# Banded attention and gated MLP on one core: convolution sums moved into PSUM, one schedule for the whole run, first probabilities turned by TensorE

## The chip, the cores and the metric

The kernel runs on one core of one Trainium2 chip. The metric is the device time of one execution in microseconds (us), lower is better. Three runs of the kernel before took 585.83, 588.0 and 584.61 us, median 585.83. Engines are called as the profile calls them: PE (TensorE; PEld its weight loads), DVE (VectorE), ACT (ScalarE), POOL (GpSimd), SP (the queue that issues all DMAs here).

## What is computed

Attention with 8 batches, 8 heads, 576 tokens and head size 64. Half of the heads see the last 32 positions, the other half the positions of equal remainder modulo 32. Its output goes through a gated MLP: 512 to 1024 features, a convolution of three taps along the tokens whose sigmoid gates the hidden value, and back to 512.

```python
scores = scale * np.matmul(q, k.transpose(0, 1, 3, 2))
scores = np.where(masks[None, :, :, :], scores, -1000000000.0)
attn = np.exp(scores - max); attn = attn / (sum + 1e-09)
x = np.matmul(attn, v)                        # heads side by side: (8, 576, 512)
h = np.maximum(x @ w_in, 0.0)                 # (8, 576, 1024)
conv_out += conv_w[k][None, None, :] * hp[:, k:k + S, :]   # k = 0, 1, 2; hp is h with a zero row at both ends
gate = 1.0 / (1.0 + np.exp(-conv_out))
return (h * gate @ w_out).astype(np.float32)
```

## The kernel before

**Attention.** Heads are worked in pairs, four pairs a batch; "head" below means such a pair. One head is: `scores` (L307, 36 small products into a PSUM tile of 128 x 576), row maximum and subtraction on DVE (L319, L320), exponential on ACT (L322), sum and reciprocal on DVE (L323, L325), scaling on POOL (L326, `pn`), a transposition of 32 x 32 blocks into `pt` (one DVE instruction for all blocks, L329, whose pieces ACT then copies to their places, L341; or DVE block by block, L344), `values` (L350, 18 products into the same PSUM tile), and a split of the result into a high part `xh` (ACT, L364) and a remainder `xl` (DVE, L365).

**MLP.** Products are made three times (high x high, high x low, low x high). `mm1` (L387) makes for each of 8 feature blocks f two halves of 288 tokens, 12 matmuls each, so 24 matmuls a block and 192 a batch. ACT clips them into `h` (L393). The convolution of a block is ACT's scaling (L398, `c`), two DVE multiply-adds (L404), ACT's sigmoid (L407), and the product with `h` (L409, DVE or in the first batch mostly POOL). The result is split into `gh` (ACT, L277) and `gl` (POOL or DVE by the string `SPLIT_G`, L280). `mm2` (L426) makes 4 x 2 output tiles out of all 8 blocks, 24 matmuls each, 192 a batch; ACT copies them out (L432) and SP stores them. So no output tile can end before the last block's `gl`.

**Weights.** The weights arrive as 64-bit words, in 16 chunks of 512 KB. Each chunk is turned into f32 by one ACT instruction (L245), five DVE instructions (L246 to L254) and one of POOL (L256), and then split into high and low (L277, L280; engine by `SPLIT_W`). `w_in` is done in the first stage and beside it, `w_out` behind it.

**Buffers.** Convolution sums `c` are three SBUF tiles. In a first stage four heads of batch 0 have four sets of attention buffers and four PSUM tiles `sF` of their own. Then that stage's pools are given back, and the second stage has two sets, two PSUM tiles `s` for attention and four `m` for matmuls. Each is a tile of its own.

**Order.** A class `Plan` records every operation with its engine, a duration, a due time and the keys that it reads and writes. `order` picks, engine by engine, the ready operation with the smallest due time, and the instructions are issued in that order, each engine in its own. The layer below (Tile) then sets the semaphore waits between engines from what each instruction reads and writes in the tiles; an engine that waits holds all that is queued behind.

Of the kernel before, what the change touches and what calls it, by code (L numbers as in the profile page):

```python
# [19 lines left out]
P = 128  # L20
# [4 lines left out]
WAIT = 0.1  # L25
ACT_PENALTY = 0
PE_PENALTY = 1

FIRST = "q0 q1 w0 q3 v1 w1 w2 q2 w3 v2 v3 c0 v0"
SETUP = ['vav', 'v', 'ava', 'v']  # L30
WARM = 4
WARM_SCORES = [2, 4, 2, 4]
WARM_VALUES = [0, 5, 0, 9]
FIRST_AT = [19.3, 22.4, 23.0, 26.9]
SECOND_AT = [11.6, 24.2, 37.3, 76.0]
LATER_AT = [31.8, 33.4, 39.2, 37.7]
START = 28.0
PERIOD = 70.0
MM1_STEP = 3.5
MM2_AT = 39.3  # L40
MM2_STEP = 22.4
LOAD_Q = 82.1
LOAD_V = 20.4
W_IN_AT = [-37.0, 3.8, 71.4, 61.1, 22.5, 42.2, 40.1, 48.5]
W_OUT_AT = [1.2, -51.9, 2.7, -37.4, 27.2, 25.2, 41.3, 30.0]
SPLIT_W = "pppppppvppvppvpv"
SPLIT_G = "vppvpppp"
FIRST_SCALE = "aavaaaav"
FIRST_GATE = "vppppvpp"


class Plan:
# [6 lines left out]
    def op(self, engine, dur, at, fn, reads=(), writes=(), chain=(), table=None):  # L59
        i = len(self.ops)  # L60
        deps = set(chain)
        for key in reads:
            if key in self.last_write:
                deps.add(self.last_write[key])
        for key in writes:
            deps.update(self.readers.get(key, ()))
            if key in self.last_write:
                deps.add(self.last_write[key])
        for key in reads:
            self.readers.setdefault(key, set()).add(i)  # L70
        for key in writes:
            self.last_write[key] = i
            self.readers[key] = set()
        deps.discard(i)
        self.ops.append((engine, dur, at, fn, deps, table))
        return i

    def order(self, free, done):
        ops = self.ops
        n = len(ops)  # L80
        left = [0] * n
        users = [[] for _ in range(n)]
        ready = [0.0] * n
        end = {}
        lo = len(done)
        for i in range(lo, n):
            for d in ops[i][4]:
                if d < lo:
                    ready[i] = max(ready[i], self.after(done[d], d, i))
                else:  # L90
                    left[i] += 1
                    users[d].append(i)
        pool = {}
        for i in range(lo, n):
            if not left[i]:
                pool.setdefault(ops[i][0], []).append(i)
        out = []
        while True:
            best = None
            for e, c in pool.items():  # L100
                if not c:
                    continue
                t = max(free.get(e, 0.0), min(ready[i] for i in c))
                def key(i):
                    sw = e == "act" and ops[i][5] not in (None, self.table) or e == "pe" and ops[i][5] != self.kind
                    return (ops[i][2] + (ACT_PENALTY if e == "act" else PE_PENALTY) * sw, i)
                cand = min((i for i in c if ready[i] <= t), key=key)
                for i in c:
                    if ready[i] > t and key(i) < key(cand) and ready[i] < t + min(WAIT, 0.9 * ops[cand][1]):
                        cand = i  # L110
                        t = ready[i]
                        break
                if best is None or t < best[0]:
                    best = (t, e, cand)
# [4 lines left out]
            if e == "act" and ops[i][5] not in (None, self.table):  # L119
                self.table = ops[i][5]  # L120
                t += 1.29
            if e == "pe" and ops[i][5] != self.kind:
                self.kind = ops[i][5]
                t += 0.087
            end[i] = t + ops[i][1]
            free[e] = end[i]
            out.append((t, i))
            for u in users[i]:
                ready[u] = max(ready[u], self.after(end[i], i, u))
                left[u] -= 1  # L130
                if not left[u]:
                    pool.setdefault(ops[u][0], []).append(u)
        out.sort()
        return [i for _, i in out], end

    def after(self, t, d, i):
        a, b = self.ops[d][0], self.ops[i][0]
        if a == "dma":
            return t + 0.92
        if b == "dma":  # L140
            return t + 1.25
        if a == b:
            return t if a == "pe" else t + 0.13
        if b == "pe":
            return t + 0.15
        return t + (0.2 if a == "pe" else 0.15 if a == "act" else 0.08 if a == "pool" else 0.2 if b == "pool" else 0.13)

    def emit(self, free, done):
        order, end = self.order(free, done)
        for i in order:  # L150
            self.ops[i][3]()
        done.extend(end[i] for i in range(len(done), len(self.ops)))
# [3 lines left out]
def tile_banded_attention_gated_mlp(ctx, tc, qT, kT, vw, w_in, conv, w_out, mask, ident, out):  # L156
# [24 lines left out]
    tt = const.tile([P, NU, 64], F32, name="tt")  # L181
# [6 lines left out]
    NW = 2  # L188
    words = [const.tile([P, 4, P, 2], I32, name=f"ws{i}") for i in range(NW)]
    wa = [const.tile([P, 4 * P], I32, name=f"wa{i}") for i in range(NW)]  # L190
    wt = [const.tile([P, 4 * P], I32, name=f"wt{i}") for i in range(NW)]
# [4 lines left out]
    def slot(n):  # L196
        return n if n < NHP else n % NB

    def load_q(n, at):
        i, b, hp = slot(n), n // NHP, HPS[n % NHP]  # L200
        q, k = buffers[i][:2]
# [357 lines left out]
```

## Time and profile before

| what | value |
|---|---|
| median of 3 runs | 585.83 us |
| the profiled execution | 583.28 us, of which 581.5 us are its span |
| DVE busy | 416.1 us (72%) |
| ACT busy | 348.6 us (60%) |
| POOL busy | 169.2 us (29%) |
| mean granted TensorE clock | 0.944 |
| HBM read, written | 41.79 MB, 9.44 MB |

The page gives busy time by engine, the span in 40 slices, the DMA queues, the chain of work that ended last, and groups of instructions by line. A group's row holds its busy time, the mean of one instruction, and the idle time of the engine just before, with what ended it. A row of the stretches ("windows") holds start and end, length, then busy time and number of instructions by engine, the granted clock, and the share and rate of DMA.

### The profile page before, as it was taken

The page shows a single profiled execution, that of the slowest core. Times are in us where ns is not written, and L with a number is a line of the kernel's source. Part 1 is how long each engine was busy: PE and PEld are TensorE (multiplying, and loading weights), DVE is VectorE, ACT ScalarE, POOL GpSimd, SP SyncE. Part 2 cuts the span into 40 slices and gives each one's busy share as a digit, 9 for nine tenths or more (in the row PEclk, how much of TensorE's full clock was granted, in tenths as well). Part 3 has the DMA queues.
Part 4 walks back from the last instruction along what each step waited for, and adds up shares of the span by engine and source line. Part 5 has one row for each costly group of instructions (what it writes and reads, how often), then busy time and mean ns, then how long its engine had stood idle before and what let it go on. Part 6 is the DMA issues. An engine that isn't in the chain of part 4 may idle for free.

```text
span 581.5 us, 15083 instructions
## 1 busy us (share of the span) xinstructions
PE 523.2 (90%) x6558; PEld 498.2 (86%) x6558; DVE 416.1 (72%) x587; ACT 348.6 (60%) x661; POOL 169.2 (29%) x148
## 2 busy tenths in 40 slices
PE   5468855798998999999999999999999999899997
PEld 2348854697997999999998999899999999799997
DVE  5596999998697666875787678767777668733830
ACT  4395685566676448663874477545765386535731
POOL 5434676674023111321033012311232103300220
PEclk9566967889999999999999999999999999999999
DMA  8994213445202460066006530355015600210001
GB/s 194 228 214 108 66 56 110 141 145 163 68 1 81 130 160 1 4 182 163 24 1 143 151 77 2 85 152 134 1 32 155 165 22 1 83 42 22 1 35 47
DMA packets 24178, 52.19 MB, mean 90 GB/s; under 512 B 2480, under 2 KB 10736, under 8 KB 24112
## 3 DMA queue, kind: packets, MB, share of 16 engines
q1 hardware_dynamic: 24112, 51.23, 33.0%
q8 instruction: 51, 0.84, 0.6%
q14 instruction: 15, 0.12, 0.1%
HBM read 41.79 MB, written 9.44 MB: 88 GB/s over the span
## 4 chain that ended last, share of the span: by engine, by line
PE 44%; DVE 22%; ACT 11%; issue 4%; POOL 0%; POOLq 0%; DVEq 0%; ACTq 0%
PE m L426 24%; PE m L387 13%; DVE c L404 8%; DVE c L409 6%; PE s L307 4%; ACT c L398 4%; ACT gh L277 2%; PE s L350 2%; ACT c L407 2%; DVE gl L280 1%; DVE wt L250 1%; DVE xl L365 1%; ACT pt L341 1%; ACT h L393 1%; ACT xh L364 1%
## 5 line engine op out<-in xcount | busy, mean ns | idle before, releaser
L387 PE MATMUL m<-xh,wil 128*128 128x288 f32 x512 | 153.1, 299 | 5.7 <-DVE wil L280 3.8
L426 PE MATMUL m<-gl,woh 128*128 128x288 f32 x512 | 153.7, 300 | 3.7 <-POOL gl L280 3.3
L426 PE MATMUL m<-gh,wol 128*128 128x288 f32 x512 | 152.6, 298 | 4.9 <-DVE wol L280 2.9
L426 PE MATMUL m<-gh,woh 128*128 128x288 f32 x512 | 155.5, 304 | 1.3 <-issue 1.3
L387 PE MATMUL m<-xh,wih 128*128 128x288 f32 x512 | 153.4, 300 | 2.0 <-DVE xl L365 1.5
L404 DVE SCALAR_TENSOR_TENSOR c<-h,cw,c 128x576 f32<-128x576 f32 x128 | 121.1, 952 | 44.7 <-ACT c L398 44.4
L387 PE MATMUL m<-xl,wih 128*128 128x288 f32 x512 | 153.1, 299 | 0.0
L280 POOL TENSOR_TENSOR gl<-c,gh 128x576 fp32r<-128x576 f32 x48 | 71.5, 1490 | 202.0 <-ACT gh L277 192.1
L426 PEld LDWEIGHTS m<-gl,woh 128*128 128x128 f32 x512 | 97.4, 190 | 9.1 <-POOL gl L280 7.5
L387 PEld LDWEIGHTS m<-xh,wil 128*128 128x128 f32 x512 | 98.2, 192 | 6.1 <-DVE wil L280 4.0
L426 PEld LDWEIGHTS m<-gh,wol 128*128 128x128 f32 x512 | 97.5, 190 | 4.0 <-DVE wol L280 3.4
L426 PEld LDWEIGHTS m<-gh,woh 128*128 128x128 f32 x512 | 97.3, 190 | 4.2 <-issue 1.5
L387 PEld LDWEIGHTS m<-xh,wih 128*128 128x128 f32 x512 | 98.2, 192 | 2.8 <-DVE xl L365 1.7
L387 PEld LDWEIGHTS m<-xl,wih 128*128 128x128 f32 x512 | 98.1, 192 | 0.0
L341 ACT COPY pt<-tt 32x288 f32<-32x288 f32 x160 | 68.8, 430 | 24.8 <-DVE tt L329 16.1
L326 POOL TENSOR_TENSOR pn<-t,sm 128x576 f32<-128x576 f32 x32 | 38.2, 1203 | 145.7 <-DVE sm L325 141.6
L277 ACT CAST gh<-c 128x576 fp32r<-128x576 f32 x64 | 43.0, 671 | 41.0 <-DVE c L409 39.3
L409 DVE TENSOR_TENSOR c<-h,c 128x576 f32<-128x576 f32 x58 | 54.7, 944 | 15.0 <-ACT c L407 14.1
L393 ACT ACTIVATE h<-m 128x288 f32<-128x288 f32 x128 | 50.5, 405 | 22.6 <-PE m L387 21.3
L432 ACT COPY o<-m 128x288 f32<-128x288 f32 x64 | 24.8, 398 | 58.5 <-PE m L426 54.2
L407 ACT ACTIVATE c<-c 128x576 f32<-128x576 f32 x64 | 43.4, 678 | 11.7 <-DVE c L404 11.0
L398 ACT ACTIVATE c<-h,cw 128x576 f32<-128x576 f32 x62 | 48.1, 775 | 1.5
(71 smaller groups left out, 590.2 us busy)
## 6 DMA issues: line engine op xcount, KB each, us to landing
v<-in_dram SPq DMA_DIRECT2D x32, 432.0 KB, 4.0
q<-in_dram SPq DMA_DIRECT2D x32, 288.0 KB, 5.0
k<-in_dram SPq DMA_DIRECT2D x32, 288.0 KB, 5.7
out_dram<-o SPq DMA_DIRECT2D x32, 288.0 KB, 2.2
ws<-in_dram SPq DMA_DIRECT2D x16, 512.0 KB, 3.7
k<-in_dram SPq DMA_DIRECT2D x1, 304.0 KB, 6.7
small<-in_dram SPq DMA_DIRECT2D x1, 32.0 KB, 2.1
cwords<-in_dram SPq DMA_DIRECT2D x1, 24.0 KB, 10.6
```

Of the source, the lines that this page charges most:

```text
L277: op(A, ta, at, lambda: nc.scalar.copy(hi(), src), [skey], [(key, "h")])
L280: lambda: eng.tensor_tensor(out=lo(), in0=src, in1=hi().bitcast(F32), op=ALU.subtract),
L326: op(G, 1.11, at + 5.5, lambda: nc.gpsimd.tensor_tensor(out=pn, in0=t, in1=sm.unsqueeze(2).to_broadcast([P, NU, 64]), op=ALU.mult), [("t", ...
L341: op(A, 0.333, at + 7.5, lambda dst=dst, j=j, p=p: nc.scalar.copy(dst, tt[j:j + 32, :, 32 * p:32 * p + 32]), ["tt"], [key])
L387: nc.tensor.matmul(ps, a[:, c, fs], x[:, c, tok], start=(n == 0 and m == 0), stop=(n == NC - 1 and m == 2))
L393: op(A, 0.291, at + 1.5 * t + 1.7, lambda ps=ps, t=t: nc.scalar.activation(out=h[:, 1 + t * H2:1 + t * H2 + H2], in_=ps, func=AF.Relu), [( ...
L398: op(A, 0.67, at + 3.6, lambda: nc.scalar.activation(out=c_, in_=h[:, 0:S], func=AF.Copy, scale=cw[:, f:f + 1]), kh + ["cw"], [kc])
L404: op(V, 0.73, at + 3.6 + 0.8 * kk, lambda kk=kk: nc.vector.scalar_tensor_tensor(out=c_, in0=h[:, kk:kk + S], scalar=cw[:, kk * NF + f:kk * ...
L407: op(A, 0.57, at + 6, lambda: nc.scalar.activation(out=c_, in_=c_, func=AF.Sigmoid), [kc], [kc], table=1)
L409: op(ge, 0.67 if ge == V else 1.36, at + 6.7, lambda: (nc.vector if ge == V else nc.gpsimd).tensor_tensor(out=c_, in0=h[:, 1:S + 1], in1=c ...
L426: nc.tensor.matmul(ps, a[:, f, ms], g[:, f, tok], start=(f == 0 and n == 0), stop=(f == NF - 1 and n == 2))
L432: op(A, 0.291, at + 3 * t + 3, lambda ps=ps, tok=tok: nc.scalar.copy(o[:, tok], ps), [("M", mi)], [("o", oi, t)])
```

## The change

1. **One PSUM tile `four`** of five banks (128 x 2560 f32) replaces the PSUM tiles of attention and the SBUF tiles `c`. It is cut into four regions of 576 columns and a spare of 256. A region is longer than a bank of 512 columns, so that neighbours share a bank. Regions 0 and 1 hold the scores and values of the heads (0 to 3 for the first batch), regions 2 and 3 by turns the convolution sums. Matmul tiles `m` fall from four to three.
2. **One schedule.** There is no first stage any more: all pools are opened at the start, attention has two sets of buffers from the first head on, and one plan covers the run. `h`, the gate's results `gt` and the output tiles lie in one SBUF tile `misc`, whose space the first three weight chunks use before.
3. **Turning by TensorE.** For the four heads of batch 0 and the first two of batch 1, POOL writes the probabilities between zero columns (`pad`), 18 matmuls with a shifted unit matrix put them transposed into PSUM, in three groups (eight into the head's region, four into the spare, six into the region again), and ACT copies each group to `pt`. L329 and eight L341 copies a head go, and the eight clearings of `pt` on POOL.
4. **The gate.** Where POOL makes the remainder, DVE writes the gate's result to SBUF (`gt`); elsewhere it stays in PSUM and DVE makes the remainder. POOL makes no gate any more.
5. **The plan** has new durations, models a port that DVE and POOL hold in turn (`lock`), the clock of TensorE and the rate of DMA, and has new due times and new strings for who splits what. It has no rule for two operations in different regions of `four`.

```diff
-FIRST = "q0 q1 w0 q3 v1 w1 w2 q2 w3 v2 v3 c0 v0"
+FIRST = "w1 w2 k0 w0 q0 q3 k1 q1 k2 v1 q2 w3 w4 c0 k3 v0 v2 v3"
...
-SPLIT_W = "pppppppvppvppvpv"
-SPLIT_G = "vppvpppp"
...
-FIRST_GATE = "vppppvpp"
+SPLIT_W = "vvpvvpvvpppvpvvv"
+SPLIT_G = "ppvvpppv"
+FIRST_SPLIT_G = "vpvppppv"
+TURNED = 2
...
+                if ops[i][6]:
+                    lock["dve"] = end[i] + 0.03
+                    lock["pool"] = end[i]
...
+    NHB, NGT, NPM = 3, 2, 3
+    misc = mlp.tile([P, NHB * (S + 2) + (NGT + 2) * S], F32, name="misc")
...
+    four = psum.tile([P, 5 * 512], F32, name="four")
+    spare = four[:, 4 * S:5 * 512]
+    psR = [four[:, S * i:S * i + S] for i in range(4)]
+    psM = [psum.tile([P, 512], F32, name=f"m{i}") for i in range(NPM)]
...
+    def region(n):
+        return n if n < NHP else n % 2
...
+    def turn(n, ps, ks, u0, n_u, key, at):
+        i = slot(n)
+        pt = buffers[i][3]
+
+        def turns():
+            for u in range(n_u):
+                for e in range(2):
+                    o = ps[0:96, 128 * u:128 * u + 128].rearrange("p (h x) -> p h x", h=2)[:, :, 32 * e:32 * e + 32]
+                    nc.tensor.matmul(o, pad[:, u0 + u, 32 - 32 * e:128 - 32 * e], unit[:, e, :], start=True, stop=True)
+        op(T, 0.112 * 2 * n_u, at, turns, ["tt", "unit"], [ks], table=3)
+        op(A, 0.25 + 0.105 * n_u, at + 0.5, lambda: nc.scalar.copy(
+            pt[:, :, u0:u0 + n_u, :].rearrange("p h u c -> p u h c"),
+            ps[0:96, 0:128 * n_u].rearrange("p (u h c) -> p u h c", h=2, c=64)), [ks], [key])
...
-        si = n if n < NHP else n % len(psum)
-        ps = psum[si][:, :S]
-        ks = ("S", si, n < NHP)
+        ps = psR[region(n)]
+        ks = ("R", region(n))
...
-        h, c_ = hs[hi], cs[hi]
+        h, gt, c_ = hs[hi], gts[gi], psR[ci]
+        sg = FIRST_SPLIT_G[f] if early else SPLIT_G[f]
...
-        kc = ("c", hi)
+        kc = ("R", ci)
...
+        if sg == "p":
+            op(V, 0.752, at + 6.7, lambda: nc.vector.tensor_tensor(out=gt, in0=h[:, 1:S + 1], in1=c_, op=ALU.mult), kh + [kc], [("gt", gi)] + old(gt0 + S * gi, S))
+            split(lambda: gh[:, f, :], lambda: gl[:, f, :], gt, at + 7.5, ("gt", gi), ("g", f), "p", 0.67, 0.752, 1.4, True)
+        else:
+            op(V, 0.752, at + 6.7, lambda: nc.vector.tensor_tensor(out=c_, in0=h[:, 1:S + 1], in1=c_, op=ALU.mult), kh + [kc], [kc])
+            split(lambda: gh[:, f, :], lambda: gl[:, f, :], c_, at + 7.5, kc, ("g", f), "v", 0.64, 0.752, 1.4, False)
```

What the built programs say of two places follows; the brackets name the semaphores for which an instruction waits, by the engine (or DMA queue) that raises them.

The first place is ACT in the convolution of a later batch. Before, the scaling of a block's neighbour (`c_541`, `c_542`) waits for ACT's own `h` and for POOL, which read that tile a batch ago:

```order
L398 ACTIVATE c_540<-h_537,cw 128x576 [waits Activation_49,Pool_49]
L393 ACTIVATE h_538<-m_552 128x288 [waits PE_49]
L407 ACT_TABLE_LOAD
L407 ACTIVATE c_540<-c_540 128x576 [waits DVE_49]
L393 ACTIVATE h_538<-m_553 128x288 [waits PE_49]
L393 ACTIVATE h_539<-m_550 128x288 [waits PE_49]
L398 ACTIVATE c_541<-h_538,cw 128x576 [waits Activation_49,Pool_49]
```

After the change the same engine stands so at that place (`misc` holds `h`, and `gt` where it is cast to `gh`):

```order
L542 ACTIVATE four<-four 128x576 [waits DVE_49]
L528 ACTIVATE misc<-m_95 128x288 [waits PE_49]
L533 ACTIVATE four<-misc,cw 128x576 [waits DVE_49]
L528 ACTIVATE misc<-m_96 128x288 [waits PE_49]
L387 CAST gh<-misc 128x576 [waits Pool_49]
L533 ACTIVATE four<-misc,cw 128x576 [waits DVE_49,Activation_49]
L528 ACTIVATE misc<-m_94 128x288 [waits PE_49]
L542 ACTIVATE four<-four 128x576 [waits DVE_49]
```

Each scaling L533 now waits for DVE: by the semaphore's value for DVE's last instruction on `four`, which worked on the other block's region. The same holds in the whole program. Taken in the order in which they are issued, the accesses to `four` change engine 399 times, and each time the later one waits, directly or through another wait, for the one ahead, whichever regions the two are in, and also where both only read.

The second place is PE in the first 30 us. Before, the scores of the four first heads stand next to each other, in tiles of their own:

```order
L307 MATMUL sF_114<-k_59,q_58 32x64 x36
L307 MATMUL sF_115<-k_67,q_66 32x64 x36
L307 MATMUL sF_117<-k_107,q_106 32x64 x36
L307 MATMUL sF_116<-k_99,q_98 32x64 x36
```

After, scores (L430) and turning matmuls (L412) alternate in `four`, and a first one of nearly each group waits for DVE or ACT:

```order
L430 MATMUL four_93<-k1_67,q1_66 32x64 [waits DMAHW1_49,DMAHW7_49,DMAHW0_49,DVE_49]
L430 MATMUL four_93<-k1_67,q1_66 32x64 x35
L412 MATMUL four_93<-unit_75,pad_74 96x2x32 [waits DMAHW2_49,Pool_49]
L412 MATMUL four_93<-unit_75,pad_74 96x2x32 x7
L430 MATMUL four_93<-k0_59,q0_58 32x64 [waits DMAHW5_49,DMAHW4_49]
L430 MATMUL four_93<-k0_59,q0_58 32x64 x35
L412 MATMUL four_93<-unit_75,pad_74 96x2x32 [waits Activation_49]
L412 MATMUL four_93<-unit_75,pad_74 96x2x32 x3
L412 MATMUL four_93<-unit_75,pad_74 96x2x32 [waits DVE_49]
```

The second head's scores wait for DVE's subtraction on the first head's region; the third and fourth groups of turning matmuls are held by ACT's copy and by DVE's maximum of other regions.

More of the change, by code (lines that the diff above doesn't have):

```diff
@@ L74, in op, with order @@
         deps.discard(i)
-        self.ops.append((engine, dur, at, fn, deps, table))
+        self.ops.append((engine, dur, at, fn, deps, table, lock))
         return i
-    def order(self, free, done):
+    def order(self, at):
         ops = self.ops
         n = len(ops)
-        left = [0] * n
-        users = [[] for _ in range(n)]
+        left = [len(o[4]) for o in ops]
+        users = self.users
         ready = [0.0] * n
[L84 to L94, printed above, removed]
-            if not left[i]:
-                pool.setdefault(ops[i][0], []).append(i)
+        pool = {e: [] for e in ("dma", "act", "dve", "pool", "pe")}
+        for i in range(n):
+            if not left[i]:
+                pool[ops[i][0]].append(i)
+        free = dict.fromkeys(pool, 0.0)
+        free["dma"] = 0.7
+        lock = {"dve": 0.0, "pool": 0.0}
+        moved = 0.0
+        idle, hot = 0.0, 0.0
+        table = kind = None
+        begin, end = [0.0] * n, [0.0] * n
@@ new lines, in best @@
+    def best(self):
+        n = len(self.ops)
+        self.users = [[] for _ in range(n)]
+        for i in range(n):
+            for d in self.ops[i][4]:
+                self.users[d].append(i)
+        rank = [o[2] for o in self.ops]
+        found = self.order(rank)
+        for _ in range(PASSES):
+            late = self.latest(rank)
+            order, begin, end = self.order(late)
+            if max(end) < max(found[2]):
+                found = order, begin, end
+            rank = end
+        return found
@@ L312, in warm_s @@
                 for _ in range(WARM_SCORES[n]):
[L313 to L316 removed]
+                    nc.tensor.matmul(psM[2][:, 288:], warm_[:, :P], warm_[:, :224], start=True, stop=True)
@@ L333, in attention @@
+        for h in range(0 if turned else 2):
             for e in range(2):
@@ new lines, in mm2, with warm_up @@
+        op(Q, 288, at + 6, lambda: nc.sync.dma_start(out=out[ms, b * S:(b + 1) * S], in_=o), [("o", oi, 0), ("o", oi, 1)], [])
+    warm_ = const.tile([P, 256], BF16, name="warm")
+    def warm_up():
+        nc.vector.memset(warm_, 0.0)
+        for _ in range(WARM):
+            nc.tensor.matmul(psM[2][:, 288:], warm_[:, :P], warm_[:, :224], start=True, stop=True)
+    with tc.manual_schedule():
+        op(T, 0.2 * WARM, -10, warm_up, (), [])
+        op(Q, 64, -19.9, lambda: nc.sync.dma_start(out=unit, in_=eye), (), ["unit"])
+        op(G, 0.4, -4.2, lambda: (nc.gpsimd.memset(pad[:, :, 0:32], 0.0), nc.gpsimd.memset(pad[:, :, 96:128], 0.0)), (), ["zero"])
+        op(Q, 32, -50, lambda: nc.sync.dma_start(out=small[D:], in_=ident), (), ["small"])
+        first = FIRST.split()
+        place = {tok: n - 20 for n, tok in enumerate(first)}
+        for j in range(NHP):
+            load_q(j, place["q%d" % j])
+            if j < NB:
+                set_up(j, place["k1"] - 0.5)
+            load_k(j, place["k%d" % j])
+            load_v(j, place["v%d" % j])
+            attention(j, FIRST_AT[j], None)
+        convert_conv(place["c0"])
+        for tok in first:
+            if tok[0] == "w":
+                convert_w_in(int(tok[1:]), W_IN_AT[int(tok[1:])], place[tok])
```

427 lines of the change are left out of this document (235 added, 192 removed).

## The prediction

> **What bounds the kernel now.** I read the share of each engine first, then the slices, then the chain that ended last.
>
> ```profile
> PE 523.2 (90%) x6558; PEld 498.2 (86%) x6558; DVE 416.1 (72%) x587; ACT 348.6 (60%) x661; POOL 169.2 (29%) x148
> PE   5468855798998999999999999999999999899997
> PEclk9566967889999999999999999999999999999999
> ```
>
> From the thirteenth slice (about 175 us) PE is full at full clock; before, it has gaps and a lowered clock. So there are two stages. The stretches give the first one's engines, and mm1's own stretches its start in batches 0 and 1.
>
> ```profile
> 30.00:40.00 10.00, 8.31 (x91) 5.80 (x93) 9.24 (x18) 9.34 (x21) 5.01 (x6) 0.53 1.00 216
> 90.00:100.00 10.00, 5.19 (x23) 4.96 (x23) 10.00 (x14) 7.14 (x13) 7.14 (x4) 0.66 0.30 84
> 230.00:300.00 70.00, 68.84 (x875) 67.11 (x874) 52.10 (x75) 44.63 (x86) 15.04 (x12) 1.00 0.29 78
> ...
> 40.00:50.00 10.00, 1.96 (x8) 1.96 (x9) 0.64 0.44 122
> 90.00:100.00 10.00, 5.19 (x23) 4.96 (x23) 0.66 0.30 84
> 140.00:150.00 10.00, 0.89 (x7) 1.01 (x8) 1.00 0.48 130
> ```
>
> At 90 us DVE is busy without a gap (weight chunks) and PE makes 23 matmuls in 5.19 us, 0.226 each, at clock 0.66. mm1 of batch 0 begins at 50 - 1.96 = 48.0, that of batch 1 at 150 - 0.89 = 149.1. From there the chain shows one period a batch:
>
> ```profile
> 214.24 12.73 PE m L387 x96
> ...
> 242.30 0.03 issue
> ...
> 244.41 0.74 DVE c L404
> 245.15 0.02 issue
> ...
> 249.32 1.58 PE s L307 x97
> ...
> 251.97 10.50 PE m L426 x78
> 262.47 2.25 PE s L350 x72
> 264.72 3.38 PE m L426 x24
> 268.11 2.15 PE s L307 x144
> 270.25 6.55 PE m L426 x48
> ...
> 525.59 12.74 PE m L387 x96
> ...
> 561.14 16.72 PE m L426 x124
> 577.86 0.02 issue
> ```
>
> mm1 starts at 214.24 and five batches later at 525.59: a period is 311.35 / 5 = 62.3 us. In it a matmul takes 12.73 / 96 = 0.1326 us, mm1 25.5. At 249.32, 35.1 us after mm1's start, the convolution of all blocks and the last `xl` are through and PE goes on; until then it has 25.5 us of mm1, 42 matmuls of mm2 (5.6) and two heads' values (2.25), so it idles some 1.8 us. Behind that point 27.5 us of PE work follow almost without a gap. **PE bounds the period; the convolution, alternating between ACT and DVE, ends just early enough.** That margin is what the change touches.
>
> The run before is thus 149.1 + (214.24 - 149.1) + 311.35 + (581.5 - 525.59) = 149.1 + 65.1 + 311.35 + 55.9 = 581.5 us, plus 1.8 outside the span.
>
> **The change, term one: a period.** After it every use of `four` by another engine waits for the use issued ahead. So a period's convolution is one chain through ACT and DVE, without the overlap of neighbouring blocks. Its pieces:
>
> ```profile
> L398 ACT ACTIVATE c<-h,cw 128x576 f32<-128x576 f32 x62 | 48.1, 775 | 1.5
> L404 DVE SCALAR_TENSOR_TENSOR c<-h,cw,c x128: 800/815/1856, 56.4 to 555.9; 128x576 f32<-128x576 f32 x128
> L407 ACT ACTIVATE c<-c x64: 667/680/691, 60.8 to 556.7; 128x576 f32<-128x576 f32 x64
> L409 DVE TENSOR_TENSOR c<-h,c x58: 742/756/1853, 62.6 to 557.4; 128x576 f32<-128x576 f32 x58
> L277 ACT CAST gh<-c x64: 657/674/679, 63.8 to 558.9; 128x576 fp32r<-128x576 f32 x64
> L280 DVE TENSOR_TENSOR gl<-c,gh x16: 746/758/1707, 66.6 to 546.6; 128x576 fp32r<-128x576 f32 x16
> L393 ACT ACTIVATE h<-m 128x288 f32<-128x288 f32 x128 | 50.5, 405 | 22.6 <-PE m L387 21.3
> ```
>
> A block whose remainder POOL makes: scaling 0.775, a multiply-add 0.815 and a second behind it 0.74 (chain), sigmoid 0.68, gate 0.756, and four hand-offs of 0.03 (the chain's "issue" rows): 3.89 us. Where DVE makes it, the cast 0.674 and the remainder 0.758 with two hand-offs join: 1.49 more. mm1 makes a block in 24 x 0.1326 = 3.18, so the chain, not mm1, sets the pace. By the new string these are blocks 2, 3 and 7. The chain begins when the first `h` is there, 3.18 + 0.405 + about 0.2 after mm1's start: 3.8. Eight blocks: 31.1; blocks 2 and 3: 3.0; gives 37.9. In block 7 a head's values or scores stand between the cast and the remainder in the issue order: 0.67 + 1.12 (2.25 / 2) + 0.76 + hand-offs with PE, say 0.3: 2.85. So the last `gl` lands **40.7 us** after mm1's start, against 35.1.
>
> What is queued behind: PE's mm2 needs block 5, 6 and 7 in turn, and PE does everything in order. The first 45 mm2 matmuls (6.0) and mm1 (25.5) fit before 40.7; PE idles there 8 us. Behind stand 147 matmuls at 10.50 / 78 = 0.1346, 19.8 us, four scores at 2.15 / 2 = 1.08 and three values at 1.12, 7.7 us, and I put 2 us for scores that wait, in `four`, for the other head's `xh` and `xl`. Sum: **70.2 us**, against 62.3 (bounds 66 and 74: the waits of the second half vanish and the values stand elsewhere, 3 to 4 less; or each of the seven costs 0.5 more). Batches 1 to 6: 6 x 70.2 = 421 against 65.1 + 311.35 = 376.5: **+45**. The last batch has no attention behind it: 3.8 + 31.1 + 3.0 + 1.5 = 39.4, then 138 matmuls (18.6) and the tail of 581.5 - 577.86 = 3.6: 61.6 against 55.9, **+6**.
>
> PSUM operands: the trace has no multiply-add on PSUM; subtracting and remaindering from PSUM take as long as from SBUF:
>
> ```profile
> L320 DVE TENSOR_TENSOR t<-s,mx 128x576 f32<-128x576 f32 x28 | 21.1, 755 | 0.7
> L365 DVE TENSOR_TENSOR xl<-s,xh 128x576 fp32r<-128x576 f32 x28 | 21.1, 754 | 25.5 <-ACT xh L364 24.8
> ```
>
> so I leave 0.815. An ACT or DVE that is 0.05 faster or slower per instruction moves the chain by 2 us, which the bounds hold.
>
> **Term two: the first stage.** Attention of batch 0 and of the first two heads of batch 1 lies in `four` too, in one chain.
>
> ```profile
> L307 PE MATMUL sF<-k,q x288: 216/254/317, 6.5 to 26.0; 128*32 128x64 f32 x144
> 50.00:60.00 10.00, 2.15 (x72) 1.91 (x72) 0.85 0.48 114
> 60.00:70.00 10.00, 1.21 (x72) 1.05 (x72) 1.00 0.16 54
> 30.00:40.00 10.00, 5.15 (x82) 4.62 (x84) 0.53 1.00 216
> ...
> L341 ACT COPY pt<-tt 32x288 f32<-32x288 f32 x160 | 68.8, 430 | 24.8 <-DVE tt L329 16.1
> ```
>
> Scores take 2.15 or 1.21 (second and third row, slow and full clock), values 5.15 x 36 / 82 = 2.26 or 1.12, maximum and subtraction 1.51, `xh` and `xl` 1.39. Turning is not in the trace: 18 matmuls, between the 18 of values (1.12) and twice 18 full-width ones at the slow clock, 36 x 0.226 = 8.1; I take 3.5 at the low clock and 2 at the full one, near the values. Its three copies lie between L341's 0.43 and `gh`'s 0.67 each; 1.5 together. Hand-offs of ten changes, many with PE, 1.2. A head: 13.5 at the low clock, 9.8 at the full. In this stage the clock was 0.50 to 0.66 before, and PE stays sparse, so I take 13.5. Four heads and two without `xh`, `xl` (12.1): 78 us. The first scores began at 6.5 us; now some 2.2 MB (three weight chunks among them) stand ahead of them in SP's queue, at 216 GB/s 10 us, so 13. mm1 of batch 0, but for single matmuls between, begins at **91** instead of 48. Then eight blocks with three DVE remainders (31.1 + 4.5), and among them two heads' `xh`, `xl`, scores (5.5) and those DVE weight instructions that stand in the chain (about 8): 49. Then the rest of mm2 and of two heads, on PE 141 x 0.1346 + 4.5 = 23.5, on DVE about 30 with five weight chunks: 28. mm1 of batch 1 begins at 91 + 49 + 28 = **168** against 149.1: +19. Bounds: all at the full clock, 13 + 56 + 43 + 24 = 136; slow turning and DVE held by POOL, 190.
>
> **What costs nothing or is hidden.** POOL loses six gates, six weight remainders and eight clearings; it is idle most of the run (29%). Three `m` tiles for four: ACT clips late by up to 0.5 us, inside PE's 8 us of waiting. Two buffer sets for four: heads 2 and 3 load only when the scores of 0 and 1 are done, beside the turning; without that cover each would cost two loads. The warm-up matmuls and the pools' border are inside the first stage's chain.
>
> **Sum.** 581.5 + 45 + 6 + 19 = 651.5, with the 1.8 outside the span 653. The profiled execution (583.28) lies 2.5 below the median of 585.83, so I forecast **655**.
>
> [...]
>
> **The rivals.**
> - *The port wins: faster.* L404 and L409 show medians of 815 and 756 ns but worst cases of 1856 and 1853, when POOL works. Their means:
>
> ```profile
> L404 DVE SCALAR_TENSOR_TENSOR c<-h,cw,c 128x576 f32<-128x576 f32 x128 | 121.1, 952 | 44.7 <-ACT c L398 44.4
> L409 DVE TENSOR_TENSOR c<-h,c 128x576 f32<-128x576 f32 x58 | 54.7, 944 | 15.0 <-ACT c L407 14.1
> ```
>
>   [...] Chance 0.06.
> - *The first stage pays for itself.* Less POOL work lets DVE finish the chunks 20 us sooner (at 90 us POOL is busy 7.14 of DVE's 10), while the periods lengthen as said: 653 - 19 - 20 = 614. Against it: DVE now stands in one chain with PE and ACT. Chance 0.12.
> - *The clock falls in every period.* PE idles in stretches of up to 3 us before blocks 5 to 7. If the clock drops as at 90 us, some 25 to 35 matmuls take 0.226 instead of 0.133, 2.3 to 3.3 us a period: 655 + 7 x 2.8 = 675. Chance 0.18.
> - *The waits don't matter* (hidden under PE entirely, nothing gained either): 583. Chance 0.02.
>
> **How the numbers follow.** The forecast has 0.62. Its own range, from periods of 66 to 74 (-25 to +23) and a first stage of 150 to 185, is about 625 to 685. With most of the clock's case and of the first stage's, 608 to 692 holds eight in ten. A measurement of this kernel tells 0.5% (3 us) from no change: faster 0.06, within 0.02, slower 0.92.
>
> **What would show it.** Right: mm1 starts 69 to 71 us apart; ACT waits on DVE for `four` (and back) in the convolution, where DVE waited on ACT 44 us in all before; no multiply-add over 0.9 us, yet a later end; PE idle about 8 us ahead of the last blocks; batch 1's mm1 near 168. Wrong: periods near 60 with PE full, or mm1 of batch 1 before 130.

## The result and the profile after

The kernel after takes 707.32 us (median of 4 runs, 704.98 to 711.32); before, measured beside it, takes 586.91. The ratio is 1.206, with a 95% interval of 1.199 to 1.213. The forecast said 655, within 608 to 692: slower was right, and the size was missed by 52 us. The profiled execution has a span of 705.8 us (581.5 before).

The page's engines, slices and shares of the chain after:

```profile
PE 582.0 (82%) x6758; PEld 544.2 (77%) x6758; DVE 392.7 (56%) x599; ACT 331.2 (47%) x626; POOL 117.5 (17%) x115
...
PE   1577788779978998888977898899878898789887
...
PEclk9955679789999999899998999899999999999999
...
PE 37%; DVE 27%; ACT 19%; issue 10%; POOL 3%; DMA 3%; SPq 1%; DVEq 0%; ACTq 0%; POOLq 0%
```

DVE and POOL do less than before (416.1 and 169.2), yet no engine is full any more: from the thirteenth slice on PE shows 7 to 9 where it had 9 in nearly every slice. That is the picture of a chain that goes from engine to engine.

The timeline of PE gives the first product of mm1 in batch 1 and in batch 7:

```profile
182.17 0.30 PE L522 MATMUL m<-xh,wih 128*128 128x288 f32 x1
...
641.99 0.29 PE L522 MATMUL m<-xh,wih 128*128 128x288 f32 x1
```

So the first stage ends at 182.2 us, six periods of (641.99 - 182.17) / 6 = 76.6 us follow, and the last batch takes 705.8 - 642.0 = 63.8. This is the measure used for every run below:

| kernel | batch 1's mm1 starts | mean period | last batch | median of runs |
|---|---|---|---|---|
| before | 149.1 | 62.7 | 56.0 | 586.91 |
| predicted | 168 | 70.2 | 61.6 | 655 |
| after | 182.2 | 76.6 | 63.8 | 707.32 |

The miss of 55 us in the span is 14 in the first stage, 6 x 6.4 = 39 in the periods, and 2 in the last batch.

The chain of waits in a later period shows the convolution of two blocks in `four` (start, duration, engine, what):

```profile
501.51 0.65 ACT four L542
...
502.18 0.83 DVE four L539
...
503.03 0.77 DVE misc L544
...
503.82 0.64 ACT four L542
...
504.49 0.76 ACT four L533
...
505.27 0.77 DVE four L547
...
509.24 0.64 ACT four L542
```

Between the sigmoid at 501.51 and its gate at 503.03 stands a multiply-add of the neighbouring block, and between the sigmoid at 503.82 and its gate at 505.27 the scaling of the next. Each step starts 0.02 to 0.03 us after the one ahead of it ends: on the sums ACT and DVE never work at the same time here. In the second half of a period the chain runs through the heads:

```profile
465.39 1.22 PE four L482 x36
...
466.64 0.77 DVE mx L441
...
467.43 0.77 DVE t L442
...
468.28 0.65 ACT xh L496
...
468.95 0.77 DVE xl L497
...
469.76 1.21 PE four L430 x72
```

PE's next scores (469.76) wait 3.1 us for four instructions of both heads. PE fills 1.8 us of that with other products and stands for 1.4. The same wait comes again at 485.60 to 488.70, and there PE stands for only 0.5 us. So PE stands for 1.9 us of the 6.3 that the two waits last together; two expectations below put the whole 6.3 down as PE standing still.

### The profile page after: what moved, and what is told of

It reads as the page before. It is cut to its first block, busy times and chain, and to the rows that moved or that the text cites. A ratio compares the mean times of both kernels' runs of the same rounds, so it can differ in the third digit from the quotient of the medians.

```text
span 705.8 us, 15489 instructions
## 1 busy us (share of the span) xinstructions
PE 582.0 (82%) x6758; PEld 544.2 (77%) x6758; DVE 392.7 (56%) x599; ACT 331.2 (47%) x626; POOL 117.5 (17%) x115
## 3 DMA queue, kind: packets, MB, share of 16 engines
q1 hardware_dynamic: 24256, 51.30, 27.5%
## 4 chain that ended last, share of the span: by engine, by line
PE 37%; DVE 27%; ACT 19%; issue 10%; POOL 3%; DMA 3%; SPq 1%; DVEq 0%; ACTq 0%; POOLq 0%
PE m L563 15%; DVE four L539 9%; PE four L482 6%; PE four L430 6%; PE m L522 6%; PE four L412 5%; ACT four L533 4%; ACT four L542 4%; DVE misc L544 3%; ACT pt L473 3%; DVE xl L497 3%; DVE t L442 2%; DVE mx L441 2%; ACT gh L387 2%; DMA q<-in_dram 2%
## 5 line engine op out<-in xcount | busy, mean ns | idle before, releaser
L563 PE MATMUL m<-gh,woh 128*128 128x288 f32 x512 | 165.1, 323 | 16.3 <-ACT gh L387 13.7
L539 DVE SCALAR_TENSOR_TENSOR four<-misc,cw,four 128x576 f32<-128x576 f32 x128 | 105.3, 822 | 60.7 <-ACT four L533 26.4
L390 POOL TENSOR_TENSOR gl<-misc,gh 128x576 fp32r<-128x576 f32 x40 | 48.3, 1206 | 244.2 <-ACT gh L387 244.2
L430 PE MATMUL four<-k,q 128*32 128x64 f32 x2304 | 45.4, 241 | 37.7 <-POOL wt L356 12.9
L430 PEld LDWEIGHTS four<-k,q 128*32 128x32 f32 x2304 | 39.7, 124 | 44.9 <-POOL wt L356 13.3
L542 ACT ACTIVATE four<-four 128x576 f32<-128x576 f32 x64 | 40.7, 636 | 52.1 <-DVE four L539 23.6
L451 POOL TENSOR_TENSOR pn<-t,sm 128x576 f32<-128x576 f32 x26 | 30.3, 1170 | 202.6 <-DVE sm L447 189.2
L473 ACT COPY pt<-pad 32x288 f32<-32x288 f32 x112 | 48.1, 430 | 25.5 <-DVE pad L454 23.7
L496 ACT CAST xh<-four 128x576 fp32r<-128x576 f32 x32 | 20.4, 638 | 84.2 <-DVE t L442 41.4
L528 ACT ACTIVATE misc<-m 128x288 f32<-128x288 f32 x128 | 51.4, 406 | 11.7 <-PE m L522 8.3
L482 PE MATMUL four<-pt,v 96*64 96x64 f32 x1152 | 47.1, 237 | 8.6 <-ACT misc L569 3.7
```

Source lines behind the costliest of these rows:

```text
L390: lambda: eng.tensor_tensor(out=lo(), in0=src, in1=hi().bitcast(F32), op=ALU.subtract),
L430: nc.tensor.matmul(ps[j:j + 32, 64 * u:64 * u + 64], q[:, h, W * s:W * s + W], k[:, h, W * s:W * s + 64], start=True, stop=True, tile_posi ...
L451: op(G, 1.152, at + 5.5, lambda: nc.gpsimd.tensor_tensor(out=pn, in0=t, in1=sm.unsqueeze(2).to_broadcast([P, NU, 64]), op=ALU.mult), [("t" ...
L473: op(A, 0.515, at + 7.5, lambda dst=dst, j=j, p=p: nc.scalar.copy(dst, tt[j:j + 32, :, 32 * p:32 * p + 32]), ["tt"], [key])
L482: nc.tensor.matmul(ps[64 * h:64 * h + 64, 64 * u:64 * u + 64], v[:, h, u, :], pt[:, h, u, :], start=True, stop=True, tile_position=(0, 64 ...
L528: op(A, 0.405, at + 1.5 * t + 1.7, lambda ps=ps, t=t: nc.scalar.activation(out=h[:, 1 + t * H2:1 + t * H2 + H2], in_=ps, func=AF.Relu), [( ...
```

## The experiments

"Starts" are the first products of mm1 of batches 1 and 7, as above; a period is a sixth of the time between them.

### No shared tile

The heads' regions and the spare become tiles of their own, and the sums go to SBUF:

```diff
-    four = psum.tile([P, 5 * 512], F32, name="four")
-    psR = [four[:, S * i:S * i + S] for i in range(4)]
+    spare = psum.tile([P, 512], F32, name="spare")
+    psR = [psum.tile([P, 1024], F32, name=f"s{i}")[:, :S] for i in range(2)]
...
-        h, gt, c_ = hs[hi], gts[gi], psR[ci]
+        h, c_ = hs[hi], gts[gi]
```

> What it does: the two heads' scores and values get a PSUM tile each, the small turning area a third, and the convolution sums go into SBUF (in the two tiles of the gate products); turning, planner, tables and loads stay as in the kernel after. Theory (every change of engine on the one tile `four` is a wait, and these waits make the period 75 to 79 us instead of 62): no wait between a block's sum and a head is left, so the starts of a batch's first products lie 62 to 66 us apart, PE no longer stands still for the other head's subtraction (6.3 us of a period after), and the multiply-adds are back at 0.95 us or more because both inputs are in SBUF; the time is 600 us (585 to 625), of which 15 to 20 us over before are the first stage. Rival (the longer period is the granted clock and the new order, not the tile): the starts stay 73 us apart or more and the time stays above 670 us.

Measured: 622.65 us, 1.063 of before (1.058 to 1.067). The starts in the timeline of PE, and then the group of multiply-adds (count, busy and mean ns of one, idle time ahead and what ended it):

```profile
171.46 0.29 PE L520 MATMUL m<-xh,wih 128*128 128x288 f32 x1
...
560.52 0.30 PE L520 MATMUL m<-xh,wih 128*128 128x288 f32 x1
```

```profile
L538 DVE SCALAR_TENSOR_TENSOR misc<-misc,cw 128x576 f32<-128x576 f32 x128 | 113.4, 896 | 32.8 <-ACT misc L532 30.1
```

The period is 64.8 us, 11.8 less than after, although a multiply-add from SBUF takes 0.896 us (the theory had 0.95 or more) where the one in PSUM took 0.822 in the kernel after. The time lies within what the theory said, the first stage at 171.5 a little above it. Of the 120 us lost, 85 come back. The tile is not the only difference, though: with the sums elsewhere the planner, its tables unchanged, sorted the operations into another order, so the 85 us are the two together. The pairs further down keep one order.

### Heads and sums in two tiles

```diff
+    four = psum.tile([P, 3 * 512], F32, name="four")
+    sums = psum.tile([P, 3 * 512], F32, name="sums")
...
+    psR += [sums[:, S * i:S * i + S] for i in range(2)]
-    NHB, NGT, NPM = 3, 2, 3
+    NHB, NGT, NPM = 3, 2, 2
```

> What it does: the one tile of five banks becomes two tiles of three banks, one for both heads and the turning area, one for both convolution sums; the mm1 and mm2 products lose one of their three banks for it, and the first batch's heads take turns in two areas. Theory (waits on the one tile): the waits between heads and sums are gone, those between the two heads and between neighbouring blocks stay; the starts lie 64 to 70 us apart and the time is 625 us (590 to 655). Were the waits between heads alone, or between blocks alone, what counts, the starts would stay at 74 us or more and the time above 680 us. Rival (clock and order): above 690 us, since the order hardly changes.

Measured: 683.7 us, 1.170 of before (1.163 to 1.177; the profile is of the longest of its four runs, 689.96). The theory's 64 to 70 us failed and the middle case came true:

```profile
171.96 0.30 PE L524 MATMUL m<-xh,wih 128*128 128x288 f32 x1
...
621.16 0.30 PE L524 MATMUL m<-xh,wih 128*128 128x288 f32 x1
```

The period is (621.16 - 171.96) / 6 = 74.9, hardly below that of after. One of the periods as a stretch (length, then PE, PEld, DVE, ACT and POOL busy, clock, DMA):

```profile
323.70:398.70 75.00, 64.57 (x819) 60.32 (x818) 44.16 (x68) 38.84 (x74) 10.58 (x10) 1.00 0.27 72
```

The clock is 1.00, so it is not what makes a period long here. What remained was the sharing among blocks, that among heads, the new order, or the bank taken from the products.

### A plan that knows the tile

```diff
+                    for x in ops[i][7]:
+                        for o, u in used.get(x, {}).items():
+                            if o != e:
+                                t = max(t, u + (0.2 if o == "pe" else 0.1 if e == "pe" else 0.06))
```

> What it does: the layout of the kernel after, untouched; only the planner gets a rule that an operation on the one tile starts after the last operation of each other engine on it, so that it sorts its order by that. Theory: the waits stay, but the order no longer issues an operation of `four` ahead of one that its own chain needs first; the starts lie 68 to 74 us apart and the time is 675 us (650 to 695): a third to a half of the loss against before is the plan's ignorance, the rest the waits themselves. Rival (the waits cost nothing, the clock does): 700 to 710 us. If the order cannot help at all because the chains alternate too often: 700 us or more as well, but then with the waits on `four` as long as after.

Measured: 704.81 us (702.72 to 710.02), as after. The starts are at 178.7 and 636.9, 76.4 apart. The theory's half on the plan fell: the planner, told of the waits and with the same due times, issues in another order and gains nothing.

### Heads share a tile, sums do not

As the first experiment, with the same order on every engine; only the two heads and the spare lie in one tile of three banks:

```diff
-    spare = psum.tile([P, 512], F32, name="spare")
-    psR = [psum.tile([P, 1024], F32, name=f"s{i}")[:, :S] for i in range(2)]
+    four = psum.tile([P, 3 * 512], F32, name="four")
+    spare = four[:, 2 * S:2 * S + 256]
+    psR = [four[:, S * i:S * i + S] for i in range(2)]
```

> What it does: as e1_two_tiles_sbuf_sums (622.65 us, starts 65 us apart), with the same order, except that the two heads and the turning area lie in one tile again; the sums stay in SBUF. Theory: here only the waits between the two heads are back; in the kernel after, PE stood 6.3 us of a period for the other head's subtraction, of which a part was ACT and DVE held by sums; so 2 to 6 us a period: starts 67 to 71 us apart, 650 us (635 to 668). Rival (waits between heads are nearly all of it): starts 74 us or more, above 685 us. Rival (they cost nothing, only heads against sums does): 622 us within 5.

Measured: 652.19 us in one run. The starts:

```profile
188.45 0.29 PE L521 MATMUL m<-xh,wih 128*128 128x288 f32 x1
...
588.85 0.30 PE L521 MATMUL m<-xh,wih 128*128 128x288 f32 x1
```

The period grows by 1.9 us to 66.7, and the first stage by 17.0 to 188.5. The time lies within the theory's 635 to 668, but by luck: the theory put 2 to 6 us into each period and did not foresee that the first stage would lose more than all periods together. Since the order is the same, this loss is the tile's alone.

### Heads and sums in one tile again

As the second experiment, with the same order on every engine and the same banks, in one tile of six banks:

```diff
-    four = psum.tile([P, 3 * 512], F32, name="four")
-    sums = psum.tile([P, 3 * 512], F32, name="sums")
+    four = psum.tile([P, 6 * 512], F32, name="four")
+    psR = [four[:, i:i + S] for i in (0, S, 1536, 1536 + S)]
```

> What it does: as e2_heads_apart_from_sums (683.7 us, starts 75 us apart, two banks for the products), with the same order and the same banks, except that heads, turning area and sums are one tile of six banks. Theory: the waits between heads and sums, which are all that is added, cost 5 to 10 us a period: starts 80 to 85 us apart, 735 us (715 to 765); then the second bank of e2 hid a gain of about that size. Rival (two banks for the products made e2 slow, and sharing between heads and sums costs nothing): 684 us within 6.

Measured: 722.03 us in one run. The starts:

```profile
183.84 0.30 PE L522 MATMUL m<-xh,wih 128*128 128x288 f32 x1
...
654.78 0.30 PE L522 MATMUL m<-xh,wih 128*128 128x288 f32 x1
```

The first stage is 11.9 us later and the period 3.6 longer (78.5), below the 5 to 10 expected; the time is within 715 to 765 because the first stage adds to it. The two regions of a kind still share a bank in both layouts; heads and sums share none in either. So a wait between heads and sums comes from the tile, not from a bank in common.

### Every second sum in SBUF

As the second experiment (two banks for the products, heads in one tile), but neighbouring blocks no longer share a tile:

```diff
-        h, gt, c_ = hs[hi], gts[gi], psR[ci]
+        h, gt = hs[hi], gts[gi]
+        c_ = gt if gi else psR[ci]
```

> What it does: as e2_heads_apart_from_sums (683.7 us, starts 75 us apart), except that the sums of every second block lie in SBUF, in the tile of its gate product; so no two neighbouring blocks share a tile, and half of the multiply-adds read two inputs from SBUF again. The products keep two banks, the heads one tile. Theory (what is left of the period in e2 is mostly neighbouring blocks that wait for each other in one tile): starts 66 to 70 us apart, 640 us (620 to 660). Rival (two banks for the products, or the heads' one tile, hold e2's period): 75 us or more, since the two SBUF inputs only add: 684 us or more.

Measured: 641.92 us in one run. The starts, and then the groups of multiply-adds of both kinds:

```profile
169.84 0.29 PE L525 MATMUL m<-xh,wih 128*128 128x288 f32 x1
...
577.84 0.30 PE L525 MATMUL m<-xh,wih 128*128 128x288 f32 x1
```

```profile
L543 DVE SCALAR_TENSOR_TENSOR misc<-misc,cw 128x576 f32<-128x576 f32 x64 | 54.9, 858 | 13.8 <-ACT misc L537 13.4
L543 DVE SCALAR_TENSOR_TENSOR sums<-misc,cw,sums 128x576 f32<-128x576 f32 x64 | 52.4, 819 | 28.7 <-ACT sums L537 28.0
```

The period falls from 74.9 to 68.0, although half of the multiply-adds are slower (0.858 us against 0.819). So two banks for the products are not what made the second experiment slow. The rest points to waits between neighbouring blocks in one tile as the largest part of the long period. That is argued and not shown, since the planner sorted the operations anew here too, and no pair with one order separates this.

### Without turning

The kernel after with the old transposition in the first two batches; then the same in the layout of the first experiment:

```diff
-            attention(j, FIRST_AT[j], None)
+            attention(j, FIRST_AT[j], [1, 1, 1, 1])
...
-                    attention(n, at, (None if j < TURNED else [1, 1, 1, 1]) if early else [1, 0, 0, 1])
+                    attention(n, at, [1, 1, 1, 1] if early else [1, 0, 0, 1])
```

> What it does: the kernel after with the old transposition in the first two batches (four 32x32 blocks on DVE and ACT and the zero fills on POOL instead of TensorE products); the one tile, tables and loads stay. Theory: the turned heads cost about 6.5 us of PE each at the low clock and wait in the one tile besides; without them the products of the second batch begin at 165 to 175 us instead of 182, the later starts stay 75 to 79 us apart, and the time is 696 us (688 to 702). Rival (the first stage is late for its loads and for the tile, not for the turning): 182 us or later, 705 us or more.

> What it does: as e1_two_tiles_sbuf_sums, with the old transposition (blocks on DVE and ACT, zero fills on POOL) in the first two batches instead of products on TensorE. Theory (turning cost 11 us in the kernel after because it stood in the one tile; with tiles apart it runs beside the rest): second batch's products at 168 to 175 as in e1, 620 us (614 to 627). Rival (turning costs PE at the low clock wherever it stands): second batch's products at 160 to 165, 612 us or less.

Measured: 693.64 and 620.63 us, one run each, against 707.32 and 622.65 with turning. Batch 1's mm1 starts at 171.4 instead of 182.2 in the one tile, and at 169.2 instead of 171.5 with tiles apart. Both theories held: turning costs 10.8 us of first stage where it stands in `four`, and where it does not, 2.3, which is little more than the 1.5 us by which the runs of the first experiment differ.

### Tiles apart, with tables sorted for them

The layout of the first experiment, with other due times, order of loads and splits; seven heads turned, the blocks of the old transposition shared out otherwise, nearly all remainders on DVE, and TensorE's cold durations in the planner's first 49 us:

```diff
-SPLIT_G = "ppvvpppv"
-FIRST_SPLIT_G = "vpvppppv"
+SPLIT_G = "vvvvvvvv"
+FIRST_SPLIT_G = "vvvvvvpv"
-FIRST = "w1 w2 k0 w0 q0 q3 k1 q1 k2 v1 q2 w3 w4 c0 k3 v0 v2 v3"
+FIRST = "w2 k2 c0 q3 w3 v3 k0 w4 q2 w0 v1 v2 k1 q0 k3 w1 q1 v0"
...
```

> What it does: the layout of e1_two_tiles_sbuf_sums (622.65 us; first products of the second batch at 171.5, starts 65 us apart), with tables of issue times, splits and loads that the planner itself sorts for this layout, seven heads turned by TensorE instead of six, remainders of all later blocks on DVE instead of POOL, and cold TensorE durations in the planner for the first 49 us. The planner's own end is 53 us earlier than with the tables of e1. Theory (e1's 37 us over before are the tables, which were sorted for a layout without port or shared tile; neither turning nor the loads as such): second batch's products at 145, starts 61 to 63 us apart, 570 us (560 to 585), faster than before. Rival (turning and the loads' order cost the first stage whatever the tables): second batch's products at 160 or later, 590 us or more.

Measured: **563.45 us**, 0.961 of before (0.957 to 0.966), the fastest kernel of this study. PE by slices, the starts, and the group of multiply-adds:

```profile
PE   0278799999999899999999899999999999999996
```

```profile
141.38 0.29 PE L530 MATMUL m<-xh,wih 128*128 128x288 f32 x1
...
507.64 0.30 PE L530 MATMUL m<-xh,wih 128*128 128x288 f32 x1
```

```profile
L548 DVE SCALAR_TENSOR_TENSOR misc<-misc,cw 128x576 f32<-128x576 f32 x128 | 102.4, 821 | 45.0 <-ACT misc L542 43.2
```

The first stage ends 7.7 us ahead of before's, a period takes 61.0, and PE is full from the sixth slice on. The multiply-adds take 0.821 us from SBUF, as long as those in PSUM (0.822 in the kernel after).

### Two parts of that kernel undone

First POOL's remainders come back (`SPLIT_G` and `FIRST_SPLIT_G` as after); then, in another kernel that keeps the order of the 563 us one on every engine, the heads go back into one tile.

> What it does: as e8_tiles_apart_new_tables (563.45 us), except that POOL makes the remainders of the blocks that it makes in the kernel after (five of eight, in the first batch six). Theory (in e8 the multiply-adds took 0.821 us from SBUF, as from PSUM in the kernel after, since POOL hardly reads while they run; with POOL's remainders they collide): multiply-adds near 0.89 us, second batch's products at 146, later starts 61 to 63 us apart, last batch 59, 576 us (569 to 584). Rival (the remainder's place does not matter, the order does): 563 us within 4.

> What it does: as e8_tiles_apart_new_tables (563.45 us) in the same order, except that the two heads and the turning area lie in one tile of three banks again. Theory (the one tile costs by itself, whatever the tables; e4 against e1 gave 17 us of first stage and 1.9 us a period): 585 us (573 to 600). Rival (it cost only because e1's tables were bad): 563 us within 4.

Measured: 573.66 and 607.02 us, one run each. The multiply-adds of the first of the two:

```profile
L548 DVE SCALAR_TENSOR_TENSOR misc<-misc,cw 128x576 f32<-128x576 f32 x128 | 107.7, 857 | 63.8 <-ACT misc L542 61.9
```

With POOL's remainders the multiply-adds slow down to 0.857 us (0.89 was expected) and the time rises by 10 us, within what was expected: batch 1's mm1 starts at 147.3 instead of 141.4 and the last batch takes 60.8 instead of 56.0; the periods stay at 60.6, since PE fills them. The order was sorted anew here, so the 10 us are not the remainders' alone. With the heads in one tile, more was lost than expected: batch 1's mm1 starts at 167.2, 25.8 us later, and a period takes 63.7, 2.6 more. In this tighter order the shared tile costs more than in the looser one (17.0 and 1.9 above); at 607 us the kernel is slower than before.

## Why the prediction was right in direction and too small

The time, 707 us, lies above the range's end of 692. Two terms of the sum were too small: the second half of a period (29.5 us put, 33.7 measured, 25 us over six periods) and the turning of the heads in the first stage (21 us put, 32.8 measured).

**Direction and mechanism: right.** The sum rested on one statement, that every use of `four` by another engine waits for the one ahead. The experiments show it in two places by pairs with one order: between heads (1.9 us a period and 17.0 in the first stage, 2.6 and 25.8 in the tighter order) and between heads and sums (3.6 a period, with what the clock adds to it, a mean of 0.935 against 0.985, and 11.9 in the first stage). Between neighbouring blocks the chain after shows the waits, one behind the other; their price, 6.9 us a period from the second experiment to every second sum in SBUF, holds a new order as well. The figures were taken from different bases, so they are not a sum.

**The convolution's chain: right in its steps, short by 2 us.** Put at 3.89 us for a block and 1.49 more where DVE splits, 5.38 together. The sigmoids of the two neighbouring blocks whose remainders DVE makes start at 503.82 and 509.24, 5.42 apart. The last `gl` was put at 40.7 us after mm1's start; counted from where mm1 stands in the chain it lands 43.3 and 42.3 after:

```profile
414.14 9.56 PE m L522 x72
...
449.65 5.65 PE m L563 x22
455.30 1.28 PE four L482 x36
...
456.68 0.77 DVE gl L390
...
457.49 6.76 PE m L563 x49
...
488.75 3.59 PE m L522 x25
...
494.56 1.28 ACT L542
...
530.32 0.77 DVE gl L390
...
531.14 6.77 PE m L563 x49
...
567.08 0.93 PE m L522 x7
```

The sum had left out, in the second of these periods, a table load of 1.28 us on ACT ahead of the first sigmoid. In the first, 22 matmuls take 5.65 us (449.65), 0.257 each at a granted clock of 0.50, ahead of the values that stand between block 7's cast and its remainder; the cast was through at 454.66, PE at 455.30, so the slow clock cost 0.6 us there. The other 2.0 of the first period's 2.6 were not traced to one wait. PE stood 5.7 and 7.0 us in these first halves (rows below), where about 8 was put.

**The second half of a period: the mis-sized term.** The prediction had 19.8 of matmuls, 7.7 of scores and values, and "2 us for scores that wait, in `four`, for the other head's `xh` and `xl`": 29.5 together. Measured, it is 31.3 and 36.0 us (457.45 to 488.75 and 531.09 to 567.08), 33.7 in the mean. The stretches of the two periods, half by half:

```profile
414.10:457.50 43.40, 37.67 (x277) 35.34 (x275) 24.55 (x33) 24.81 (x47) 6.77 (x6) 0.92 0.02 8
457.50:488.80 31.30, 29.40 (x481) 27.64 (x481) 14.68 (x25) 12.09 (x24) 2.31 (x2) 1.00 0.51 133
488.80:531.10 42.30, 35.34 (x300) 32.93 (x300) 25.00 (x35) 24.55 (x46) 7.18 (x6) 0.96 0.06 16
531.10:567.10 36.00, 31.11 (x579) 28.84 (x580) 22.14 (x38) 14.71 (x29) 4.61 (x4) 1.00 0.57 144
```

(length, then PE, PEld, DVE, ACT and POOL busy, clock.) In the second halves PE stands 3.4 us in the mean, against 2 in the sum, and is busy for 30.3, against 27.5, with about the same work: 530 matmuls, where the sum had 147 products, four scores of 72 and three values of 36, 543. So 1.4 of the 4.2 us are standing and 2.8 a longer busy time. The first of these halves holds two waits of 3.1 us (466.62 to 469.72, quoted above, and 485.60 to 488.70), in which scores wait for the maximum and subtraction of one head and the `xh` and `xl` of the other; the sum had put only the last two, and as a lump. Scores that stand alone take 1.21 us at 469.76, where the sum had 1.08, half of the 2.15 of two that stand together; that such longer times of work cut into pieces by the waits are all of the 2.8 is argued from these rows and was not measured by itself. The second half is 4.2 of the 6.4 us by which a period was missed, the first half 2.1.

**The first stage: turning was mis-sized.** Put at 3.5 us a head at the low clock, 21 for the six heads. The group of turning matmuls after (all six heads, with the idle time of PE ahead of them), the last values of these heads on PE, and the last remainder of batch 0's convolution on DVE:

```profile
L412 PE MATMUL four<-unit,pad 128*96 128x64 f32 x216 | 32.8, 328 | 19.5 <-ACT pt L414 4.4 <-DVE t L442 4.3 <-POOL pad L451 3.9
```

```profile
102.81 1.27 PE L482 MATMUL four<-pt,v 96*64 96x64 f32 x36
```

```profile
153.91 0.74 DVE L390 TENSOR_TENSOR gl<-four,gh 128x576 fp32r<-128x576 f32 x1
```

Turning took 32.8 us, 11.8 more than put. The heads' chain was to end at 91 and ended at 104.1, 13 later; the first scores, at 14.87 instead of 13, are 2 of it. The two parts behind it came out as put: the convolution of batch 0 took 50.6 us from there (49 put), and 27.5 more led to batch 1's mm1 (28 put). So the chain of the heads is nearly all of the 14 us by which this stage was missed. That does not make it the only limit: with the old transposition the heads' chain ends at 76.6, 27.5 us earlier, but batch 1's mm1 starts only 10.8 earlier, at 171.4. In both kernels the last remainder of `w_out` is made 3 to 4 us ahead of that start (at 179.0 and 167.6), so the weights may be what takes up the rest; that was not tested.

**PSUM operands: right.** The multiply-add was left at 0.815 and none was to exceed 0.9; the mean was 0.822 and the longest 0.825. Not worth what it costs here: with POOL's remainders gone, 0.821 is to be had from SBUF. With both inputs in SBUF a multiply-add took 0.896 us in the first experiment and 0.857 in the 563 us kernel with POOL's remainders, and 0.821 in the 563 us kernel itself, where DVE makes 63 of the 64 remainders; with every second sum in SBUF the two kinds stand in one run, 0.858 with both inputs in SBUF and 0.819 with the sum in PSUM.

**The rivals.** The relief of the multiply-adds was real (0.952 us in the mean before, 0.822 after), but it lies off the path: in a period PE's products decide as soon as the tile is apart (61.0 and 60.6 us with multiply-adds of 0.821 and 0.857). The clock did fall in every period, to 0.95 to 0.98 in the mean of each of the six (1.00 in all six of before) and to 0.92 and 0.96 in the first halves above, as the third rival had it; but there the convolution's chain ends later than PE or nearly so (0.6 us above), and the second experiment had a period of 74.9 at a clock of 1.00. So the clock is a small part of the long period; how small was not measured by itself. That the first stage would pay for itself fell: it grew by 33 us.

**Tile and bank.** In the second experiment and its one-tile twin heads and sums share no bank. In the twin the waits between heads and sums came nevertheless (3.6 us a period, 11.9 in the first stage): the tile decides here. The two heads, and two neighbouring blocks, share a bank wherever they share a tile, so for them tile and bank are not told apart.

**What stays open.** The first experiment is 37 us slower than before with no tile shared. The tables account for it, since other tables in that layout give 563.45; which of them (due times, loads, the seventh head, the cold durations) does how much was not taken apart, but that POOL's remainders, with the order that goes with them, cost 10 us. No run keeps the order of the kernel after and takes its tile apart, so how much of the 120 us is the tile and how much its order stays open as well.

## What to carry to other kernels

Where tiles are put into one PSUM tile to save banks, count the changes of engine on it in the order of issue: each was a wait here, whatever region or bank it touched, and independent chains that shared an order become one chain. A tuned order is tuned for the waits that its planner knows; here neither a faster instruction nor a planner that was told of the waits brought back what the shared tile took, while tiles apart with an order sorted for them won 4% over the start. Before sums are moved to PSUM to make DVE's multiply-adds faster, see what POOL does beside them: with nearly all remainders on DVE they took the same 0.82 us from SBUF.

## What the runs showed of the hardware

In the first experiment PE stands once a batch, six times between the first products of batches 1 and 7 and 14.1 us in all, until DVE has made another head's remainder `xl`. One such wait in the timeline, and the stretches around it (length, then PE, PEld, DVE, ACT and POOL busy, clock, DMA):

```profile
341.78 0.98 PE L429 MATMUL s<-k,q 128*32 128x64 f32 x28 [2.35 <-DVE xl L496]
```

```profile
336.00:339.00 3.00, 3.00 (x109) 2.75 (x109) 1.98 (x4) 1.88 (x3) 0.00 (x0) 1.00 0.00 0
339.00:342.00 3.00, 0.65 (x26) 0.52 (x23) 2.72 (x5) 2.50 (x4) 1.24 (x1) 0.96 0.84 194
342.00:345.00 3.00, 3.00 (x77) 2.83 (x70) 1.78 (x4) 0.68 (x1) 0.12 (x1) 0.50 0.77 155
345.00:348.00 3.00, 3.00 (x24) 3.00 (x24) 1.67 (x3) 1.68 (x4) 1.15 (x1) 0.97 0.89 207
```

After 2.35 us without work the clock is 0.50 from 342 to 345 us, and 0.97 in the 3 us behind. A wait of this length did not lower it each time. Two neighbouring stretches of the same run, and a wait of 2.57 us in the 563 us kernel with the stretch around it:

```profile
239.00:303.00 64.00, 61.57 (x819) 60.04 (x819) 44.07 (x67) 38.94 (x74) 10.30 (x8) 1.00 0.33 85
303.00:368.00 65.00, 62.65 (x817) 61.15 (x817) 44.82 (x68) 38.89 (x74) 11.46 (x9) 0.97 0.32 83
```

```profile
318.95 0.29 PE L572 MATMUL m<-gh,woh 128*128 128x288 f32 x1 [2.57 <-issue]
```

```profile
264.50:327.70 63.20, 60.63 (x817) 59.72 (x817) 48.72 (x76) 38.92 (x72) 4.54 (x4) 1.00 0.33 86
```

PE stands for 2.43 us in the first of the two, at a clock of 1.00, and for 2.35 in the second, which holds the wait above, at 0.97. In the 563 us kernel the clock stayed at 1.00 over the stretch with the 2.57 us. What made the difference was not shown.
